# The opening of a fused linear-attention and two-layer kernel: weight tiles loaded and decoded earlier, the first block's products moved behind the last attention units

## The chip, the cores and the metric

One core of one Trainium2 chip. The metric is the device time of one execution in microseconds (us). The kernel before took 906.34, 907.86 and 909.46 us in three runs; the median is 907.86 us.

## The reference

Decayed linear attention over 4 sequences, 8 heads, 768 positions, 64 per head; its rows go through two layers, each with a nonlinearity between two matrix products.

```
for t in range(S):
    state = gamma * state + einsum('bhd,bhe->bhde', k[:, :, t], v[:, :, t])
    y[:, :, t] = scale * einsum('bhd,bhde->bhe', q[:, :, t], state)
x = y.transpose(0, 2, 1, 3).reshape(3072, 512)
h = x @ w_in                  # 512 x 2048
x = (h - tanh(h)) @ w_out     # 2048 x 512
h = x @ w_in2                 # 512 x 1024
solu = h * softmax(h)
out = layer_norm(solu) * g_ln @ w_out2
```

Weights arrive as float64 and are turned into float32 pairs (high and low part) on the core.

## The kernel before

**Attention.** Positions are cut into 6 chunks of 128; with 4 sequences that makes 24 units, number k = 4 x chunk + sequence. A unit has two input tiles of 512 KB, `z` (`load_half`, L194: first q and k, then k and v), which SP issues; SP also issues the weight tiles and the decay tables `tab` (L190). `prepare(k)` scales q on POOL (L223) and v partly on ACT (L230, one instruction a head) and partly on POOL (L234). `unit(ko, ks)` then does on PE the products "out" of unit ko and "sc" of unit ks (both L211, 64x64 matmuls), and on DVE and ACT what follows: the mask and the running state (L305, L311 to L316), the sum `xf` (ACT L277 to L281, DVE L285), and `split_x`, which cuts xf into a high part (ACT, L323) and a low part (DVE and POOL, L324).

**First layer.** Four units of one chunk make one block of 512 rows. `step_h(n, b)`, called h(n,b) here, multiplies column tile n of w_in (16 tiles) with block b: `products_h` issues 12 matmuls of 128x512 (L337), `less_tanh` follows (ACT L344, DVE L345). h(n,b) needs weight tile n, decoded, and all four units of block b.

**Decoding a weight tile.** `Decoder.to(stage, upto)`: stage 0 is the load (`raw`, 512 KB, L120), stage 1 an absolute value on ACT (L126), stage 2 four operations on DVE (L133, L134, L137, L140), stage 3 a copy on ACT (L149) and a subtraction on DVE (L150).

**What sets the order.** The code is written once, in program order, and a scheduler (in the tile framework) may move an instruction on its engine, except where `pin` keeps it in program order. Before, `pin` holds the unit matmuls, the first two blocks' h matmuls and some ACT copies of units 0 to 7. The matmuls of the opening stand on PE in this order: sc(0), sc(1), out(0), sc(2), out(1), sc(3), out(2), sc(4), out(3), sc(5), out(4), sc(6), h(0,0), out(5), sc(7), out(6), h(1,0), out(7), and then, without units between, h(0,1), h(1,1), h(2,0), h(2,1), h(3,0), h(3,1). From then on unit 8 to 11 (the third block) are strewn between the steps of the loop `for n in range(NF1)`, first sc(8), and after h(15,1) `products_y` (L362) starts on the second matrix. It needs `split_g(0)`, which cuts g of tile 0 into high (ACT, L350) and low part.

In the loop `for k in range(2 * B)` weight tile 0 is decoded in the code of units 1 and 2, tile 1 in that of units 4 and 5:

```
        if k in (1, 4):
            for st in (1, 2):
                dec1.to(st, 1 + (k > 1))
        elif k in (2, 5):
            dec1.to(3, 1 + (k > 2))
        if k in (4, 6):
            step_h((k - 4) // 2, 0)
```

Of the kernel before, what the change touches and what calls it, by code (L numbers as in the profile page):

```python
# [90 lines left out]
def body(ctx: ExitStack, tc, z, w_in, w_out, w_in2, w_out2, g_ln, cst, tab, out):  # L91
# [29 lines left out]
        return raw  # L121


    def stage1(raw):
        wf = t2([P, 512], F32, "wf")
        nc.scalar.activation(wf, raw[:, :, 1].bitcast(F32), AF.Abs)  # L126
        return wf

    def stage2(raw, wf):

        hw, lw = raw[:, :, 1], raw[:, :, 0]
        wb = wf.bitcast(I32)
        nc.vector.tensor_scalar(wf, wf, W_MIN, W_MAX, ALU.max, ALU.min)  # L133
        nc.vector.tensor_scalar(  # L134
            wb, wb, 3, 0x3FFFFFF8, ALU.logical_shift_left, ALU.bitwise_and
        )
        nc.vector.scalar_tensor_tensor(  # L137
            wb, lw, 29, wb, ALU.logical_shift_right, ALU.bitwise_or
        )
        nc.vector.scalar_tensor_tensor(  # L140
            wb, hw, -0x40000000, wb, ALU.bitwise_and, ALU.bitwise_or
        )

    def stage3(wf, scale, eng):
# [4 lines left out]
        nc.scalar.copy(hi, wf)  # L149
        eng.tensor_tensor(lo, wf, hi.bitcast(F32), ALU.subtract)  # L150
        return hi, lo

    class Decoder:
# [2 lines left out]
            self.at = [0] * 4  # L156
            self.raw, self.wf, self.w = {}, {}, {}

        def to(self, st, upto):
            while self.at[st] < min(upto, self.n):  # L160
                i = self.at[st]
                if st == 0:
                    self.raw[i] = raw_load(self.srcs[i])
                elif st == 1:
                    self.wf[i] = stage1(self.raw[i])
                elif st == 2:
                    stage2(self.raw.pop(i), self.wf[i])
                else:
                    self.w[i] = stage3(self.wf.pop(i), self.scales[i], self.eng)
                self.at[st] += 1  # L170

        def step(self):
# [40 lines left out]
    def prepare(k, own, wide=False):  # L213

        c = k // B
        if wide:
            t = t4([P, 2, H * D], F32, "vq")
            v = t[:, 0, :].rearrange("q (h d) -> q h d", h=H)
            qs[k] = t[:, 1, :].rearrange("q (p t) -> q p t", p=NP)
        else:  # L220
            v = t2([P, H, D], F32, "vs")
            qs[k] = t2([P, NP, P], F32, "qs")
        nc.gpsimd.tensor_tensor(  # L223
            qs[k].rearrange("q p t -> q (p t)"),
            zq[k][:, 0, :, :].rearrange("q p t -> q (p t)"), tb[c], ALU.mult,
        )
        src = zv[k][:, 1, :, :].rearrange("q p (h d) -> q (p h) d", h=2)
        c0 = C_VS + c * H
        for h in range(own):
            pin(nc.scalar.activation(  # L230
                v[:, h, :], src[:, h, :], AF.Copy, scale=con[:, c0 + h : c0 + h + 1]
            ), wide)
        if own < H:
            nc.gpsimd.tensor_tensor(  # L234
                v[:, own:, :], src[:, own:, :],
                con[:, c0 + own : c0 + H].unsqueeze(2).to_broadcast([P, H - own, D]), ALU.mult,
            )
        vs[k] = v

    def unit(ko, ks, hold=False, pool=ps_r, tag="r", engs=None, amid=None):  # L240
# [4 lines left out]
        if ko is not None:  # L245
# [36 lines left out]
            if amid:  # L282
                amid()
            for ab in steps:
                nc.vector.tensor_tensor(  # L285
                    xa[:, :, rows(ab)], xa[:, :, rows(ab)], ya[ab], ALU.add
                )
            if not hold:
                split_x(c, b, xf, engs or (nc.gpsimd, nc.gpsimd), amid)
        if ks is not None:  # L290
# [11 lines left out]
            ])  # L302
            pr = t2([P, 2, NP, D], F32, "pr")
            for h in range(2):
                nc.vector.tensor_tensor(  # L305
                    pr[:, h, :, :], sc[h], mask.unsqueeze(1).to_broadcast([P, NP, D]), ALU.mult
                )
# [10 lines left out]
    def split_x(c, b, xf, engs, fixed=False):  # L318
        if b == 0:
            xt[c] = [[t4([P, 2, SB], F32R, f"x{n}") for _ in range(2)] for n in "hl"]  # L320
        for h in range(2):
            xh, xl = (xt[c][n][h][:, :, b * P : (b + 1) * P] for n in range(2))
            pin(nc.scalar.copy(xh, xf[:, h, :, :]), fixed)  # L323
            engs[h].tensor_tensor(xl, xf[:, h, :, :], xh.bitcast(F32), ALU.subtract)  # L324


    gt = {}
# [88 lines left out]
    nc.scalar.dma_start(out=con, in_=cst[:, :C_IDENT])  # L416
    load_half(0, 1)
    loaded[0] = 1
    load_units(3)
    dec1.to(0, 1)  # L420
    load_units(6)
    dec1.to(0, 2)
    load_units(2 * B)
    for k in range(2):
        prepare(k, H // 2, True)
        unit(None, k, **spare)
    prepare(2, H // 2, True)

    def ahead(k):
# [3 lines left out]
    for k in range(2 * B):  # L433
        both = (nc.vector, nc.gpsimd) if k < 2 * B - 1 else (nc.vector, nc.vector)
        unit(
            k, k + 2 if k + 2 < 2 * B else None, engs=both,
            amid=lambda: ahead(k + 3), **spare
        )

        if k in (1, 4):  # L440
            for st in (1, 2):
                dec1.to(st, 1 + (k > 1))
        elif k in (2, 5):
            dec1.to(3, 1 + (k > 2))
# [29 lines left out]
    gs = {}  # L474

    def split_g(n):
        g = g2.pop(n)
        gs[n] = [split(g[:, b, :], nc.scalar, nc.vector) for b in range(2)]
# [213 lines left out]
```

## Time and profile before

| | us |
|---|---|
| median of three runs | 907.86 |
| the profiled execution | 906.58 |
| its span, first to last instruction | 904.8 |
| PE busy | 875.7 (97%) |
| DVE busy | 434.4 (48%) |
| ACT busy | 301.5 (33%) |
| POOL busy | 192.9 (21%) |

A row of the timeline has the start in us, the time from the start of the first to the end of the last of its instructions, the engine, the line, the operation, the tile written and those read, the shape and the count; in brackets the idle time of the engine before it and what ended it. "issue" there is time in which the engine waited for nothing that the profile shows. The table by stretch gives busy times (and the number of instructions) of PE, PE's weight loads (PEld), DVE, ACT and POOL, then the granted clock of PE, the mean busy share of the 16 DMA engines and GB/s. A row "q8" is the queue that the profile names "instruction".

### The profile page before, as it was taken

What the parts mean: (1) busy time and instruction counts of PE and PEld (TensorE: products, weight loads), DVE (VectorE), ACT (ScalarE), POOL (GpSimd) and SP (SyncE); (2) the same over time, 40 slices, a digit from 0 to 9 for tenths busy, and PEclk for the clock granted to TensorE, in tenths of its full rate; (3) what the DMA queues carried; (4) which work ended last, traced back from release to release, by engine and by line L of the source; (5) the groups of instructions that cost most, each with busy time, mean ns of one, the idle gap of its engine ahead of it and who ended that gap; (6) DMA issues with size and microseconds to landing.
All of it is one profiled execution on the core that took longest, in us unless ns stands there. A gap on an engine that the chain in (4) does not pass through costs nothing.

```text
span 904.8 us, 15888 instructions
## 1 busy us (share of the span) xinstructions
PE 875.7 (97%) x6656; PEld 723.9 (80%) x6656; DVE 434.4 (48%) x873; ACT 301.5 (33%) x606; POOL 192.9 (21%) x200
## 2 busy tenths in 40 slices
PE   4689999999999999999999999999999999999998
PEld 4577887888888887888788888888888888888886
DVE  2877857992232223222322269954544444444442
ACT  4446435551111111111111143622444333333332
POOL 4410000000233433333333210011222121222210
PEclk9799999999999999999999999999999999999999
DMA  9943104340312113110401055114111111100000
GB/s 360 342 168 120 35 24 158 98 137 27 94 67 75 60 47 94 48 47 7 134 6 44 24 151 175 48 35 129 47 36 38 44 47 46 36 24 24 24 24 35
DMA packets 34775, 71.93 MB, mean 79 GB/s; under 512 B 3088, under 2 KB 15504, under 8 KB 34704
## 3 DMA queue, kind: packets, MB, share of 16 engines
q1 hardware_dynamic: 18288, 58.01, 19.0%
q10 hardware_dynamic: 16416, 12.91, 4.5%
q8 instruction: 52, 0.85, 0.4%
q14 instruction: 19, 0.16, 0.1%
HBM read 58.32 MB, written 12.58 MB: 78 GB/s over the span
## 4 chain that ended last, share of the span: by engine, by line
PE 93%; DMA 3%; DVE 1%; issue 1%; ACT 1%; POOL 1%; SPq 0%; POOLq 0%; ACTq 0%
PE ph L337 29%; PE py L362 29%; PE po L616 15%; PE ph L568 14%; PE ptr L603 2%; PE out L211 2%; PE sc L211 2%; DMA z<-z 2%; DMA y1d<-ysb 1%; POOL qs L223 0%; DVE xl L324 0%; POOL vs L234 0%; DVE wf L140 0%; DVE w L150 0%; ACT th L344 0%
## 5 line engine op out<-in xcount | busy, mean ns | idle before, releaser
L362 PE MATMUL py<-gh,w 128*128 128x512 f32 x768 | 248.8, 392 | 1.2 <-ACT gh L350 1.2
L337 PE MATMUL ph<-xh,w 128*128 128x512 f32 x768 | 247.8, 392 | 2.0 <-ACT xh L323 2.0
L337 PEld LDWEIGHTS ph<-xh,w 128*128 128x128 f32 x768 | 145.1, 189 | 32.9 <-ACT xh L323 2.2
L362 PEld LDWEIGHTS py<-gh,w 128*128 128x128 f32 x768 | 143.4, 188 | 31.8 <-ACT gh L350 1.6
L345 DVE TENSOR_TENSOR g<-ph,th 128x512 f32<-128x512 f32 x96 | 66.3, 691 | 183.7 <-ACT th L344 183.7
L337 PE MATMUL ph<-xl,w 128*128 128x512 f32 x384 | 150.3, 391 | 0.3 <-DVE xl L324 0.3
L362 PE MATMUL py<-gl,w 128*128 128x512 f32 x384 | 149.8, 390 | 0.0
L344 ACT ACTIVATE th<-ph 128x512 f32<-128x512 f32 x96 | 57.3, 598 | 264.4 <-PE ph L337 248.9
L568 PE MATMUL ph<-w,y 128*128 128x512 f32 x576 | 134.9, 389 | 0.0
L353 POOL TENSOR_TENSOR gl<-g,gh 128x512 fp32r<-128x512 f32 x48 | 61.8, 1287 | 334.8 <-DVE gh L352 301.2
L568 PEld LDWEIGHTS ph<-w,y 128*128 128x128 f32 x576 | 108.1, 188 | 22.4
L616 PE MATMUL po<-w,uh 128*128 128x512 f32 x384 | 120.4, 395 | 0.0
L397 POOL TENSOR_TENSOR y<-yl,y 128x512 fp32r<-128x512 f32 x24 | 42.2, 1760 | 260.9 <-ACT y L396 232.5
L574 DVE TENSOR_REDUCE nmx<-ph 128x1 f32<-128x1024 f32 x24 | 29.4, 1225 | 117.7 <-PE ph L568 117.7
L337 PEld LDWEIGHTS ph<-xl,w 128*128 128x128 f32 x384 | 72.5, 189 | 15.5 <-DVE xl L324 0.6
L362 PEld LDWEIGHTS py<-gl,w 128*128 128x128 f32 x384 | 72.1, 188 | 14.9
L616 PEld LDWEIGHTS po<-w,uh 128*128 128x128 f32 x384 | 70.6, 188 | 13.6
L616 PE MATMUL po<-w,ul 128*128 128x512 f32 x192 | 75.3, 392 | 0.0
L577 ACT ACTIVATE ex<-ph,nmx 128x1024 f32<-128x1024 f32 x24 | 26.8, 1117 | 132.5 <-DVE nmx L574 132.5
L579 DVE SCALAR_TENSOR_TENSOR ex<-ph,ex 128x1024 f32<-128x1024 f32 x24 | 29.4, 1225 | 29.8 <-ACT ex L577 29.8
L616 PEld LDWEIGHTS po<-w,ul 128*128 128x128 f32 x192 | 36.0, 188 | 7.6
L149 ACT CAST w<-wf 128x512 fp32r<-128x512 f32 x48 | 29.6, 618 | 29.6 <-DVE wf L140 29.4
(76 smaller groups left out, 844.4 us busy)
## 6 DMA issues: line engine op xcount, KB each, us to landing
z<-z SPq DMA_DIRECT2D x48, 512.0 KB, 5.2
raw<-w_in SPq DMA_DIRECT2D x24, 512.0 KB, 5.0
raw<-w_out SPq DMA_DIRECT2D x24, 512.0 KB, 3.7
y1d<-ysb ACTq DMA_DIRECT2D x24, 256.0 KB, 3.5
yl<-y1d SPq DMA_DIRECT2D x24, 256.0 KB, 3.2
out<-ob ACTq DMA_DIRECT2D x24, 256.0 KB, 2.2
tab<-tab SPq DMA_DIRECT2D x5, 256.0 KB, 4.1
tab<-tab ACTq DMA_DIRECT2D x1, 256.0 KB, 4.6
```

What stands on the lines that cost most here:

```text
L149: nc.scalar.copy(hi, wf)
L211: pin(nc.tensor.matmul(o, a, b, start=True, stop=True, skip_group_check=True))
L337: nc.tensor.matmul(ph, a[:, k, :], x, start=n == 0, stop=n == 3 * NK - 1), s < 2
L344: nc.scalar.activation(th, ph, AF.Tanh)
L345: nc.vector.tensor_tensor(g, ph, th, ALU.subtract)
L353: eng_l.tensor_tensor(gl_, g, gh.bitcast(F32), ALU.subtract)
L362: nc.tensor.matmul(py[e], a[:, cols], x, start=f == 0 and n == 0, stop=f == NF1 - 1 and n == 2)
L397: nc.gpsimd.tensor_tensor(yo, t, yh.bitcast(F32), ALU.subtract)
L568: nc.tensor.matmul(ph[:, half, :], a[:, k, :], b, start=n == 0, stop=n == 3 * NK - 1)
L574: nc.vector.tensor_reduce(nmx, phf, AX.X, ALU.max, negate=True)
L579: nc.vector.scalar_tensor_tensor(ex, phf, 1.0, ex, ALU.mult, ALU.mult, accum_out=us)
L616: nc.tensor.matmul(po, a[:, f, :], b, start=n == 0, stop=n == 3 * NF2 - 1)
```

## The change

- **SP:** both weight tiles are loaded right behind the z tiles of units 0 and 1 (before: tile 0 behind unit 2's, tile 1 behind unit 5's). Tiles 2 and 3 are loaded where they were, behind the last z tile and two tables.
- **Decoding** of tile 0 stands behind sc(1) and in the code of unit 0, that of tile 1 in the code of units 0 and 1. Tile 2 is decoded, now pinned, in the code of unit 7.
- **h(0,0) and h(1,0)** stand behind out(6) and out(7).
- **`pin`** now also holds the POOL operations, the DVE operations and the decoding of units 0 to 7, so that ACT, DVE and POOL keep the program order there, as PE does.
- **The third block:** `prepare(k + 1)` now stands behind `unit(k)`, and that of unit 8 one step earlier, at n = 2. The loads of its z tiles move with it.
- **`split_g(0)`** stands before h(15,·) and no longer behind h(15,1).

```diff
-        nc.gpsimd.tensor_tensor(
+        pin(nc.gpsimd.tensor_tensor(
             qs[k].rearrange("q p t -> q (p t)"),
             zq[k][:, 0, :, :].rearrange("q p t -> q (p t)"), tb[c], ALU.mult,
-        )
+        ), wide)
...
-                nc.vector.tensor_tensor(
+                pin(nc.vector.tensor_tensor(
                     xa[:, :, rows(ab)], xa[:, :, rows(ab)], ya[ab], ALU.add
-                )
+                ), amid)
...
-            engs[h].tensor_tensor(xl, xf[:, h, :, :], xh.bitcast(F32), ALU.subtract)
+            pin(engs[h].tensor_tensor(xl, xf[:, h, :, :], xh.bitcast(F32), ALU.subtract), fixed)
...
-    load_units(3)
-    dec1.to(0, 1)
-    load_units(6)
+    load_units(2)
     dec1.to(0, 2)
     load_units(2 * B)
     for k in range(2):
         prepare(k, H // 2, True)
         unit(None, k, **spare)
+    for st in (1, 2):
+        dec1.to(st, 1, True)
     prepare(2, H // 2, True)
...
-        if k in (1, 4):
-            for st in (1, 2):
-                dec1.to(st, 1 + (k > 1))
-        elif k in (2, 5):
-            dec1.to(3, 1 + (k > 2))
-        if k in (4, 6):
-            step_h((k - 4) // 2, 0)
-    for st, n in enumerate((4, 3, 3, 3)):
-        dec1.to(st, n)
+        if k == 0:
+            for st, n in ((3, 1), (1, 2), (2, 2)):
+                dec1.to(st, n, True)
+        elif k == 1:
+            dec1.to(3, 2, True)
+        elif k >= 2 * B - 2:
+            if k == 2 * B - 1:
+                dec1.to(0, 4)
+                for st in (1, 2, 3):
+                    dec1.to(st, 3, True)
+            step_h(k - (2 * B - 2), 0)
...
     for n in range(NF1):
         while dec1.at[3] < n + 1:
             dec1.step()
+        if n == NF1 - 1:
+            split_g(0)
         for b in range(2):
             if n > 1 or b:
                 step_h(n, b)
 
-        if LATER <= n <= LATER + B:
-            k = 2 * B + n - LATER
-            if n == LATER:
-                load_units(k + 1)
-                prepare(k, H)
-            load_units(min(k + 2, 3 * B))
-            if n < LATER + B - 1:
-                prepare(k + 1, H)
-            unit(k - 1 if n > LATER else None, k if n < LATER + B else None, True)
+        k = 2 * B + n - LATER
+        if 2 * B <= k <= 3 * B:
+            unit(k - 1 if k > 2 * B else None, k if k < 3 * B else None, True)
+        if 2 * B <= k + 1 < 3 * B:
+            load_units(min(k + 3, 3 * B))
+            prepare(k + 1, H)
...
-    split_g(0)
```

The queue of SP at the start, the rows of before with -, those of the change with + (z and raw are 512 KB each):

```order
-L194 DMA z<-z 128x1024 x6
-L120 DMA raw<-w_in 128x1024
-L194 DMA z<-z 128x1024 x2
+L194 DMA z<-z 128x1024 x4
+L120 DMA raw<-w_in 128x1024 x2
+L194 DMA z<-z 128x1024 x4
 L190 DMA tab<-tab 128x512
-L194 DMA z<-z 128x1024 x4
-L120 DMA raw<-w_in 128x1024
-L194 DMA z<-z 128x1024 x4
```

The z tiles of unit 2 now stand as seventh and eighth, behind two weight tiles; those of unit 3 one place later than before, those of units 6 and 7 where they were.

PE, the first rows that differ; they stand behind sc(6) and lead into out(5) (sa and sb are a unit's states):

```order
 L211 MATMUL out<-pr,vq 64x64 x16
 L211 MATMUL sc<-vq,z 64x64 x32
-L337 MATMUL ph<-xh,w 128x512
-L337 MATMUL ph<-xl,w 128x512
-L337 MATMUL ph<-xh,w 128x512 x2
-L337 MATMUL ph<-xl,w 128x512
-L337 MATMUL ph<-xh,w 128x512 x2
-L337 MATMUL ph<-xl,w 128x512
-L337 MATMUL ph<-xh,w 128x512 x2
-L337 MATMUL ph<-xl,w 128x512
-L337 MATMUL ph<-xh,w 128x512
 L211 MATMUL out<-vq,sa 64x64 x4
```

h(0,0) is gone from here and stands behind out(6), where h(1,0) was; h(1,0) now follows out(7) and runs into h(0,1). All other matmuls up to sc(8) keep their order.

ACT around the scalings of v for units 8 and 9 (vs, L230), before:

```order
L149 CAST w<-wf 128x512
L230 ACTIVATE vs<-z,con 128x64 x16
L126 ACTIVATE wf<-raw 128x512
L344 ACTIVATE th<-ph 128x512 x2
L230 ACTIVATE vs<-z,con 128x64 x8
L277 COPY xc<-out 128x256 x2
```

and with the change:

```order
L149 CAST w<-wf 128x512 x2
L230 ACTIVATE vs<-z,con 128x64 x8
L126 ACTIVATE wf<-raw 128x512
L344 ACTIVATE th<-ph 128x512 x2
L230 ACTIVATE vs<-z,con 128x64 x8
L149 CAST w<-wf 128x512
```

The sixteen scalings in a row are parted: unit 8's eight stand two tanh (L344, one per h) ahead of unit 9's.

## Rows read from the trace of the kernel before

**Rows 1.** Table by stretch: from:to, length, busy times, clock, DMA share, GB/s.

```profile
15.75:21.80 6.05, 2.76 (x126) 2.45 (x127) 1.85 (x5) 4.01 (x16) 4.44 (x6) 1.00 1.03 407
21.80:27.99 6.19, 3.36 (x127) 3.17 (x126) 5.93 (x8) 1.39 (x5) 5.10 (x5) 0.72 1.02 394
27.99:32.08 4.09, 3.21 (x111) 2.83 (x111) 3.03 (x6) 3.63 (x15) 3.29 (x4) 0.63 0.52 122
32.08:40.85 8.77, 8.74 (x268) 7.74 (x268) 7.32 (x20) 4.92 (x16) 1.47 (x2) 0.78 0.96 381
```

**Rows 2.** Timeline of PE: where it resumes after being idle in the opening.

```profile
15.76 0.29 PE L211 MATMUL sc<-vq,z 64*64 64x64 f32 x4 [1.61 <-issue]
21.81 0.28 PE L211 MATMUL sc<-vq,z 64*64 64x64 f32 x3 [3.00 <-issue]
28.00 0.28 PE L211 MATMUL out<-vq,sb 64*64 64x64 f32 x4 [2.83 <-issue]
32.09 0.38 PE L211 MATMUL out<-vq,sb 64*64 64x64 f32 x4 [0.86 <-DVE sb L313]
44.81 0.29 PE L211 MATMUL out<-vq,sb 64*64 64x64 f32 x4 [3.99 <-issue]
```

**Rows 3.** The page: PE's instructions; the queue q8 (packets, MB, share).

```profile
PE 875.7 (97%) x6656; PEld 723.9 (80%) x6656; DVE 434.4 (48%) x873; ACT 301.5 (33%) x606; POOL 192.9 (21%) x200
...
q8 instruction: 52, 0.85, 0.4%
```

**Rows 4.** DMA queues in 19.3:19.4, 29.1:29.2 and 36.4:36.5 us (share of 16 engines).

```profile
q8 instruction: 1, 0.02, 64.1%
...
q8 instruction: 1, 0.02, 86.5%
...
q8 instruction: 1, 0.02, 61.8%
```

**Rows 5.** The chain of waits: start, us, what.

```profile
45.86 4.54 PE ph L337 x12
50.40 1.11 PE out L211 x64
...
54.31 16.41 PE ph L337 x71
```

**Rows 6.** Timeline of SP.

```profile
23.06 6.83 SPq L190 DMA_DIRECT2D tab<-tab  x2
29.94 3.75 SPq L120 DMA_DIRECT2D raw<-w_in  x6
```

**Rows 7.** Timeline of POOL and ACT: scalings that wait for z tiles.

```profile
10.63 1.27 POOL L223 TENSOR_TENSOR vq<-z,tab 128x512 f32<-128x512 f32 x1 [0.67 <-DMA z<-z]
15.99 1.27 POOL L223 TENSOR_TENSOR vq<-z,tab 128x512 f32<-128x512 f32 x1 [3.47 <-DMA z<-z]
28.27 1.27 POOL L223 TENSOR_TENSOR vq<-z,tab 128x512 f32<-128x512 f32 x1
17.23 1.06 ACT L230 ACTIVATE vq<-z,con 128x64 f32<-128x64 f32 x4 [2.87 <-DMA z<-z]
```

**Rows 8.** Timeline of PE around sc(8) and sc(9), and ACT's row before sc(8).

```profile
70.63 0.69 PE L211 MATMUL sc<-qs,z 64*64 64x64 f32 x32
72.20 2.01 PE L211 MATMUL sc<-vs,z 64*64 64x64 f32 x32 [0.88 <-ACT vs L230]
74.14 0.50 PE L337 MATMUL ph<-xh,w 128*128 128x512 f32 x1
...
80.78 0.66 PE L211 MATMUL sc<-qs,z 64*64 64x64 f32 x32
...
81.84 0.50 PE L337 MATMUL ph<-xh,w 128*128 128x512 f32 x1
...
71.80 3.93 ACT L230 ACTIVATE vs<-z,con 128x64 f32<-128x64 f32 x16
```

**Rows 9.** Timeline of PE: the first matmul on the second matrix.

```profile
149.18 1.20 PE L362 MATMUL py<-gh,w 128*128 128x512 f32 x4 [1.19 <-ACT gh L350]
```

More of the change, by code (lines that the diff above doesn't have):

```diff
@@ L121, in raw_load, with stage1, stage2, stage3 @@
         return raw
-    def stage1(raw):
+    def stage1(raw, fixed):
         wf = t2([P, 512], F32, "wf")
-        nc.scalar.activation(wf, raw[:, :, 1].bitcast(F32), AF.Abs)
+        pin(nc.scalar.activation(wf, raw[:, :, 1].bitcast(F32), AF.Abs), fixed)
         return wf
-    def stage2(raw, wf):
+    def stage2(raw, wf, fixed):
         hw, lw = raw[:, :, 1], raw[:, :, 0]
         wb = wf.bitcast(I32)
-        nc.vector.tensor_scalar(wf, wf, W_MIN, W_MAX, ALU.max, ALU.min)
-        nc.vector.tensor_scalar(
+        pin(nc.vector.tensor_scalar(wf, wf, W_MIN, W_MAX, ALU.max, ALU.min), fixed)
+        pin(nc.vector.tensor_scalar(
             wb, wb, 3, 0x3FFFFFF8, ALU.logical_shift_left, ALU.bitwise_and
-        )
-        nc.vector.scalar_tensor_tensor(
+        ), fixed)
+        pin(nc.vector.scalar_tensor_tensor(
             wb, lw, 29, wb, ALU.logical_shift_right, ALU.bitwise_or
-        )
-        nc.vector.scalar_tensor_tensor(
+        ), fixed)
+        pin(nc.vector.scalar_tensor_tensor(
             wb, hw, -0x40000000, wb, ALU.bitwise_and, ALU.bitwise_or
-        )
-    def stage3(wf, scale, eng):
+        ), fixed)
+    def stage3(wf, scale, eng, fixed):
         w = t4([P, 2, 512], F32R, "w")
@@ L148, in stage3 @@
             nc.scalar.activation(wf, wf, AF.Copy, scale=scale)
-        nc.scalar.copy(hi, wf)
-        eng.tensor_tensor(lo, wf, hi.bitcast(F32), ALU.subtract)
+        pin(nc.scalar.copy(hi, wf), fixed)
+        pin(eng.tensor_tensor(lo, wf, hi.bitcast(F32), ALU.subtract), fixed)
         return hi, lo
@@ L157, in __init__, with to @@
             self.raw, self.wf, self.w = {}, {}, {}
-        def to(self, st, upto):
+        def to(self, st, upto, fixed=False):
             while self.at[st] < min(upto, self.n):
@@ L164, in to @@
                 elif st == 1:
-                    self.wf[i] = stage1(self.raw[i])
+                    self.wf[i] = stage1(self.raw[i], fixed)
                 elif st == 2:
-                    stage2(self.raw.pop(i), self.wf[i])
+                    stage2(self.raw.pop(i), self.wf[i], fixed)
                 else:
-                    self.w[i] = stage3(self.wf.pop(i), self.scales[i], self.eng)
+                    self.w[i] = stage3(self.wf.pop(i), self.scales[i], self.eng, fixed)
                 self.at[st] += 1
@@ L222, in prepare @@
             qs[k] = t2([P, NP, P], F32, "qs")
-        nc.gpsimd.tensor_tensor(
+        pin(nc.gpsimd.tensor_tensor(
             qs[k].rearrange("q p t -> q (p t)"),
             zq[k][:, 0, :, :].rearrange("q p t -> q (p t)"), tb[c], ALU.mult,
-        )
+        ), wide)
         src = zv[k][:, 1, :, :].rearrange("q p (h d) -> q (p h) d", h=2)
@@ L233, in prepare @@
         if own < H:
-            nc.gpsimd.tensor_tensor(
+            pin(nc.gpsimd.tensor_tensor(
                 v[:, own:, :], src[:, own:, :],
                 con[:, c0 + own : c0 + H].unsqueeze(2).to_broadcast([P, H - own, D]), ALU.mult,
-            )
+            ), wide)
         vs[k] = v
@@ L284, in unit @@
             for ab in steps:
-                nc.vector.tensor_tensor(
+                pin(nc.vector.tensor_tensor(
                     xa[:, :, rows(ab)], xa[:, :, rows(ab)], ya[ab], ALU.add
-                )
+                ), amid)
             if not hold:
@@ L304, in unit @@
             for h in range(2):
-                nc.vector.tensor_tensor(
+                pin(nc.vector.tensor_tensor(
                     pr[:, h, :, :], sc[h], mask.unsqueeze(1).to_broadcast([P, NP, D]), ALU.mult
-                )
+                ), amid)
             pt[ks] = pr
@@ L438, in body, with split_g @@
         )
-        if k in (1, 4):
-            for st in (1, 2):
-                dec1.to(st, 1 + (k > 1))
-        elif k in (2, 5):
-            dec1.to(3, 1 + (k > 2))
-        if k in (4, 6):
-            step_h((k - 4) // 2, 0)
-    for st, n in enumerate((4, 3, 3, 3)):
-        dec1.to(st, n)
+        if k == 0:
[9 more added lines that the diff above has]
+            step_h(k - (2 * B - 2), 0)
     nc.sync.dma_start(out=gl, in_=g_ln)
+    gs = {}
+    def split_g(n):
+        g = g2.pop(n)
+        gs[n] = [split(g[:, b, :], nc.scalar, nc.vector) for b in range(2)]
     for n in range(NF1):
@@ L473, in body @@
                 dec1.to(st, max(NF1 if st < 3 else min(NF1, n + 2), NF1 + ahead[m]))
[L474 to L478, printed above, removed]
-    split_g(0)
     dec1.to(0, NF1 + 4)
```

## The prediction

> **What bounds the kernel now.** I read the page first: PE is busy for 97% of the span [rows 3]. A change of order can only win where PE idles, or works below its full clock of 2.4 GHz (granted 0.63 to 0.78 between 21.8 and 40.85 us, so partly at 1.2 GHz [rows 1]), and both stand before 54 us. From 54.31 us on, 71 matmuls of 128x512 run without a break [rows 5]. So the question is when that unbroken stretch begins, and what is left open behind it.
>
> The chain of waits names the decoding of tile 0 on DVE between 24 and 30 us, and one expects that moving it frees those 6 us. The timeline of PE says otherwise. It stops four times for "issue", that is, for no semaphore: it resumes at 15.76, 21.81, 28.00 and 44.81 us after 1.61, 3.00, 2.83 and 3.99 us, 11.4 us in all [rows 2]. For DVE it waits once, 0.86 us, until 32.09 [rows 2]. The table by stretch tells what the four stops have in common. From 15.75 to 21.80 PE and PEld start 126 + 127 instructions, from 21.80 to 27.99 127 + 126, and from 27.99 to 40.85, over two stretches, 222 + 536 = 758, which is three times 253 [rows 1]. The page has 6656 + 6656 of them and 52 packets of the queue "instruction", 0.85 MB: 256 to a packet [rows 3]; the few that are missing from 253 are PE's waits, which are not counted. So PE's program comes in blocks of 256 instructions by the same 16 DMA engines that carry z and w_in, and PE stops where a block is not there yet.
>
> The time for one block can be read. The block that PE resumed with at 15.76 us was the last it had; the next packet starts in 19.3:19.4 and takes 64.1% of 0.1 us x 16 engines = 1.03 us [rows 4], so it ends at 20.4, and PE goes on at 21.81, 1.4 us later. Wait of 3.6, packet 1.03, 1.4 until it runs: 6.05 us, and 6.19 for the next [rows 1]. That is with the DMA engines full (share 1.03, 1.02). After 28.00 they are half empty (share 0.52) [rows 1], and the packet starts in 29.1:29.2, after 1.1 us, and takes 86.5% = 1.38 us [rows 4]: 1.1 + 1.38 + 1.4 = 3.9 us. The following block is entered just after 32.09, and its packet starts at 36.4 and takes 61.8% = 0.99 us: 4.3 + 0.99 + 1.4 = 6.7 us, the longest, with the loads of w_in tiles (from 29.94 us [rows 6]) in front of it [rows 4]. So a block costs 6.1 us behind a full DMA, 3.9 behind a quiet one.
>
> The Trainium skill ("Runtime: NRT & Kernel Launch", "Instruction fetch mechanics") says that instructions come in 16 KiB blocks of 256 by a DMA queue of the sequencer, and calls the cost of crossing into a block mostly hidden. The size agrees with [rows 3]; hidden it is not in [rows 2]. What the time would be if it were hidden is the third rival.
>
> **The change, part by part.** Units 0 to 7 need about the same number of blocks in any order, so I follow the blocks.
>
> 1. *Two weight tiles ahead of unit 2.* Unit 2's q half landed ahead of 10.63, unit 3's ahead of 15.99 [rows 7]. The tiles land in the order of the queue, so unit 2's second half now takes the place of unit 3's q half, 15.95 us. The second block is entered within sc(2), at the product that needs unit 2's fourth scaling on ACT; four take 1.06 us [rows 7], so at 17.05 instead of 15.76: **+1.3 us on the chain of blocks**.
> 2. *The next blocks.* 17.05 + 6.1 + 6.1 = 29.25 us: the bytes ahead of the last z tile are the same, so the DMA goes quiet where it did (share 0.52 from 27.99 on [rows 1]), and now stays quiet for longer. SP's second table waits for the slot that POOL's scaling for unit 7 frees. Before, that scaling ran at 28.27 [rows 7], the second table was out by 29.9 and the w_in tiles went from 29.94 [rows 6]. Now POOL keeps program order, so unit 7's scaling stands behind the low parts of units 2 and 3 (L324), which wait for out(2) and out(3), that is for the blocks entered at 23.15 and 29.25. I put the w_in loads at about 35 us. So two blocks at 3.9: 33.1 and 37.0 us. The sixth is asked for at 37.0, 2 us after those loads start: 6.1 us, **43.1 us**; bounds 3.9 (40.9 us) and 6.7 (43.7 us). Before, this block came at 44.81.
> 3. *h(0,0) and h(1,0).* As now for h(1,0), the rest of the out products takes 1.05 us (44.81 to 45.86), then h(0,0) runs, out(7) 1.11, h(1,0), and h(0,1) begins. Twelve matmuls take 2.77 us in the unbroken stretch (16.41 / 71 each) and took 4.54 behind the idle of 3.99 us [rows 5]; as PE idles as long again, I take 4.54 for h(0,0) and 2.77 for h(1,0), which also covers the chain of unit 7 (51.51 to 54.31 before). 43.1 + 1.05 + 4.54 + 1.11 + 2.77 = 52.6 us. Before, the stretch of 72 began, in effect, one matmul ahead of 54.31, at 54.1. **Gain 1.5 us**; bounds: 40.9 and h(0,0) at 2.77 gives 48.6, gain 5.5; 43.7 gives 53.2, gain 0.9.
> 4. *Decoding.* Tile 0 now is turned while DVE waits for unit 2's z, tile 1 beside units 0 and 1; neither has a reader before 43 us. Nothing on the path: the 0.86 us that DVE held PE at 32.09 [rows 2] is within the wait for the block. Tile 2 is needed at h(2,0), 5.5 us after h(0,1) begins; its load comes some 10 us before. Its ACT and DVE operations, some 5 us with the two tanh steps among them, start with the end of unit 7's chain, so they fit with little to spare; if not, the cost is that difference.
> 5. *Unit 8.* Now sc(8) takes from 70.63 to 74.14, 3.5 us, and sc(9) from 80.78 to 81.84, 1.06 us [rows 8]: sc(8) stops 0.88 us for ACT and then goes at the pace of 16 scalings in 3.93 us [rows 8]. With eight of them one step earlier they lie beside h matmuls: **gain 2.45 us**. Bound below: 0.88 alone if ACT is late again.
> 6. *split_g(0) earlier.* PE waits 1.19 us for gh [rows 9]. Ahead of h(15,·) the split has 5.5 us of cover. **Gain 1.2 us.**
> 7. *Order held on ACT, DVE, POOL.* It costs what stands behind a waiting instruction; the only place where I see this decide is POOL's scaling in step 2, and there it delays SP's w_in loads, which have time.
>
> Sum: 1.5 + 2.45 + 1.2 = 5.15 us. Against the profiled execution, 906.58 - 5.15 = 901.4; against the median of 907.86, 902.7. The profiled run lies low in the three (906.34 to 909.46); I take 902.0.
>
> **The rivals.**
>
> - *The sixth block is asked for before the w_in loads fill the engines*, and h(0,0) may run at the unbroken pace. For it: the table and the loads start within some 2 us of the request, either side. Gain 5.5 with both (3.7 with the first alone), in all 7.4 to 9.2 us: about 899.
> - *Nothing of the opening is won:* the two blocks from 29 to 37 us cost 6.1, because other bytes keep the engines busy. 17.05 + 5 x 6.1 = 47.55 us, 2.75 after now's 44.81 instead of 1.7 before it: h(0,1) at 57.0, loss 2.9, less 3.65 for steps 5 and 6: 905.8 to 907.1, no change. Against it: share 0.52 in the stretch that follows the last z [rows 1].
> - *The blocks are hidden after all* and "issue" was something that the new order does not meet. Then the last z tile bounds: unit 7's scaling can't end before 29.5, two blocks of PE work behind it at the pace of 32.08 to 40.85 less h(0,0) (about 2.8 us each [rows 1]) give 35.2 in place of 43.1: 7.9 us more, 894.
> - *Slower:* the two weight tiles in front put PE behind by one block's place, and every block up to h(0,0) then costs the longest 6.7 us [rows 4]: 17.05 + 5 x 6.7 = 50.55, h(0,1) at 60.0, loss 5.9 less 3.65 = 2.3, against the median 910.1. It decides from 6.2 us a block on (each tenth is 0.5 us); above 6.8 it would be plainly slower. For it: one block did cost 6.7. Against: four did not.
>
> **How the numbers follow.** A measurement here can tell 0.3%, 2.7 us. My forecast has 0.5, the first rival 0.27, the hidden blocks 0.04, nothing won 0.13, slower 0.06. The range reaches from the first rival's better end (907.86 - 9.2 less what the runs spread, 897) to the third case (906): it leaves out the hidden blocks, the slower case and the ends. Faster by over 0.3% (below 905.1) is the forecast, the first rival and the hidden blocks, with a little of the forecast's upper end lost: 0.8. Same 0.15, slower 0.05.
>
> **What would show it.** PE resumes after "issue" at about 17, 23, 29, 33, 37 and 43 us, with 253 counted instructions between; SP issues w_in tiles 2 and 3 near 35 us, not 30; h(0,0) starts near 44 and h(0,1) near 52; sc(8) takes about 1 us and no gap stands before the first L362. Wrong is the account of the opening if PE's stops end with a semaphore of DVE, POOL or ACT, if their distance is not 256 instructions, or if h(0,1) begins before 47 or after 55 us.

## The result and the profile after

| | before | after |
|---|---|---|
| median, us | 908.44 (4 runs, 906.34 to 909.46) | 900.16 (4 runs, 898.75 to 900.99) |
| ratio, 95% interval | | 0.991 [0.9887, 0.9933] |
| profiled execution, us | 906.58 | 900.99 |
| its span, us | 904.8 | 899.2 |

The kernel became 8.3 us faster by the medians (6 to 10 us by the interval) and 5.6 by the profiled executions. The forecast was 902.0 in a range from 897 to 906. The page of after has the same instructions and the same 52 packets of PE's program as [rows 3]; only PE's span has shrunk.

```profile
span 899.2 us, 15890 instructions
...
PE 874.1 (97%) x6656; PEld 723.5 (80%) x6656; DVE 434.1 (48%) x873; ACT 301.4 (34%) x606; POOL 193.8 (22%) x200
...
q8 instruction: 52, 0.85, 0.4%
```

The timeline of PE in the opening of after, the rows with idle time ahead of them, answers to [rows 2]:

```profile
14.75 1.23 PE L211 MATMUL sc<-vq,z 64*64 64x64 f32 x32 [2.35 <-POOL vq L223]
16.14 1.52 PE L211 MATMUL sc<-vq,z 64*64 64x64 f32 x29 [0.16 <-ACT vq L230]
22.52 0.28 PE L211 MATMUL sc<-vq,z 64*64 64x64 f32 x3 [1.89 <-issue]
27.32 0.38 PE L211 MATMUL out<-vq,sb 64*64 64x64 f32 x9 [2.82 <-ACT sb L311]
28.87 0.38 PE L211 MATMUL out<-vq,sb 64*64 64x64 f32 x4 [1.16 <-issue]
35.96 0.27 PE L211 MATMUL out<-vq,sa 64*64 64x64 f32 x1 [0.41 <-issue]
41.95 0.37 PE L211 MATMUL out<-vq,sa 64*64 64x64 f32 x2 [3.87 <-issue]
```

The table by stretch between these rows, with the columns of [rows 1]: PE and PEld start 127 + 126, twice 254 and 126 + 127 instructions, so 253, two times 254, and 253, as the blocks of 256 want it. The two blocks from 28.87 cost 7.09 us together with the DMA engines at a share of 0.06, the next one 5.99 us at 0.98. PE is busy for 6.60 of the 7.09 us, at a granted clock of 0.60, so these two blocks lie near PE's own pace; the price of a quiet block is read better from the second execution of this kernel (after2, below).

```profile
22.52:28.87 6.35, 2.37 (x127) 2.10 (x126) 5.52 (x11) 3.68 (x15) 2.95 (x4) 0.91 0.93 355
28.87:35.96 7.09, 6.60 (x254) 6.28 (x254) 5.13 (x15) 5.50 (x22) 5.70 (x7) 0.60 0.06 18
35.96:41.95 5.99, 2.13 (x126) 1.99 (x127) 4.16 (x12) 1.66 (x5) 1.46 (x2) 0.95 0.98 339
41.95:49.72 7.77, 7.77 (x121) 6.25 (x120) 1.60 (x4) 1.96 (x5) 2.02 (x2) 0.60 1.02 408
```

The chain of waits of after, which answers to [rows 5] and [rows 8]: h(0,0) from 43.50 at a low clock, out(7), and then 84 matmuls (h(1,0), and h(0,1) to h(3,1)) without a break up to sc(8), which now takes 1.09 us.

```profile
38.09 3.87 issue
41.95 1.54 PE out L211 x31
43.50 5.13 PE ph L337 x12
48.63 1.09 PE out L211 x64
49.72 19.28 PE ph L337 x84
69.00 1.09 PE sc L211 x64
```

sc(8) stands at 69.00 where it stood at 70.63 [rows 8]: 1.63 us are won ahead of it. The h matmuls behind it go on at 70.09 in place of 74.14: 2.4 us more. From there to the first L362 it is 73.51 us (70.09 to 143.60, row below) in place of 75.04 (74.14 to 149.18): 1.5 us less, of which 1.19 are the wait for gh [rows 9]. Behind that both take 755.6 us to the end. 1.6 + 2.4 + 1.5 = 5.6 us, all of it.

```profile
143.60 1.52 PE L362 MATMUL py<-gh,w 128*128 128x512 f32 x6
```

SP's queue in after, which answers to [rows 6]: the w_in tiles go out at 35.21 us.

```profile
22.88 12.28 SPq L190 DMA_DIRECT2D tab<-tab  x2
35.21 2.33 SPq L120 DMA_DIRECT2D raw<-w_in  x5
```

### The profile page after: what moved, and what is told of

Read it like the earlier page. It is cut to its first block, busy times and chain, and to the rows that moved or that the text cites. A ratio compares the mean times of both kernels' runs of the same rounds, so it can differ in the third digit from the quotient of the medians.

```text
span 899.2 us, 15890 instructions
## 1 busy us (share of the span) xinstructions
PE 874.1 (97%) x6656; PEld 723.5 (80%) x6656; DVE 434.1 (48%) x873; ACT 301.4 (34%) x606; POOL 193.8 (22%) x200
## 4 chain that ended last, share of the span: by engine, by line
PE 94%; DMA 2%; issue 1%; DVE 1%; ACT 1%; POOL 1%; ACTq 0%; POOLq 0%
PE ph L337 29%; PE py L362 29%; PE po L616 15%; PE ph L568 15%; PE out L211 3%; PE ptr L603 2%; PE sc L211 2%; DMA z<-z 1%; DMA con<-cst 1%; DMA y1d<-ysb 0%; POOL qs L223 0%; POOL vs L234 0%; DVE g L345 0%; ACT th L344 0%; DVE w L150 0%
## 5 line engine op out<-in xcount | busy, mean ns | idle before, releaser
L362 PE MATMUL py<-gh,w 128*128 128x512 f32 x768 | 248.8, 392 | 0.0
L362 PEld LDWEIGHTS py<-gh,w 128*128 128x128 f32 x768 | 143.3, 188 | 30.4 <-ACT gh L350 0.2
L362 PE MATMUL py<-gl,w 128*128 128x512 f32 x384 | 149.8, 390 | 0.0
L344 ACT ACTIVATE th<-ph 128x512 f32<-128x512 f32 x96 | 57.3, 598 | 258.9 <-PE ph L337 245.9
L362 PEld LDWEIGHTS py<-gl,w 128*128 128x128 f32 x384 | 72.1, 188 | 14.9
L353 DVE TENSOR_TENSOR gl<-g,gh 128x512 fp32r<-128x512 f32 x48 | 33.8, 707 | 10.1 <-PE py L362 8.1
```

Of the source, the lines that this page charges most:

```text
L344: nc.scalar.activation(th, ph, AF.Tanh)
L353: eng_l.tensor_tensor(gl_, g, gh.bitcast(F32), ALU.subtract)
L362: nc.tensor.matmul(py[e], a[:, cols], x, start=f == 0 and n == 0, stop=f == NF1 - 1 and n == 2)
```

## The experiments

The theory: PE's program comes in blocks of 256 instructions by the DMA engines that carry z and w_in, and the gain of the opening comes from when those engines are quiet. The main rival: PE waits for data (tile 0's decoding, unit 7's chain), and the weight tiles that come earlier are what is won. p_unit8, p_split, p_open and a_h0 ran on one chip, after2, a_dup, a_quiet and a_both on a second, a_nopin, a_loads and a_best on a third, a_ql apart from these; the kernel before ran beside each group, and kernels of different groups are compared by their ratios to it. In the tables and timelines of kernels with added lines, the line numbers shift by one or two.

**The three parts alone.** Each kernel has one part of the change.

p_unit8, the kernel before with the new order of the third block:

```diff
-            load_units(min(k + 2, 3 * B))
-            if n < LATER + B - 1:
-                prepare(k + 1, H)
-            unit(k - 1 if n > LATER else None, k if n < LATER + B else None, True)
+            unit(k - 1 if k > 2 * B else None, k if k < 3 * B else None, True)
+        if 2 * B <= k + 1 < 3 * B:
+            load_units(min(k + 3, 3 * B))
+            prepare(k + 1, H)
```

> The kernel before with only the third block's order of the change (prepare behind the unit, unit 8's one step earlier). Theory: sc(8) takes about 1.06 us instead of 3.5, the opening stays as before (PE's stops of the opening at the same times within 0.3 us): 2.45 us less than the kernel before. Rival (the moved loads and scalings collide with the decoding of the w_in tiles): only the 0.88 us that sc(8) waited for ACT, or less.

Measured: ratio 0.9979 [0.9969, 0.9989], 1.9 us less. sc(8) starts both halves 0.51 us apart and has no wait:

```profile
70.71 0.69 PE L211 MATMUL sc<-qs,z 64*64 64x64 f32 x32
71.22 0.65 PE L211 MATMUL sc<-vs,z 64*64 64x64 f32 x32
```

The opening, though the same as before's, does not repeat within the 0.3 us that I expected: its stops end at 16.15, 22.42, 28.69 and 45.06 us, 0.25 to 0.7 us behind [rows 2]. So much can two executions differ there.

p_split, the kernel before with split_g(0) ahead of h(15,·):

```diff
+        if n == NF1 - 1:
+            split_g(0)
...
-    split_g(0)
```

> The kernel before with only split_g(0) ahead of h(15,.). Theory: the 1.19 us wait for gh ahead of the first L362 is gone and nothing else moves: 1.2 us less than the kernel before. Rival (the split delays tanh and the subtraction of h(14,.), so that PE waits for a free ph there): 0 us, with a new gap of PE ahead of h(15,.).

Measured: ratio 0.9993 [0.9983, 1.0004]: 0.6 us less, with 1.2 and 0 both inside the interval. Its trace has the first L362 at 147.86 us in place of 149.18, directly behind the h matmuls, which gives the theory's size; the medians can't tell it from nothing.

p_open, the changed kernel with these two undone:

```diff
-        if n == NF1 - 1:
-            split_g(0)
...
-        if 2 * B <= k + 1 < 3 * B:
-            load_units(min(k + 3, 3 * B))
-            prepare(k + 1, H)
+            load_units(min(k + 2, 3 * B))
+            if n < LATER + B - 1:
+                prepare(k + 1, H)
+            unit(k - 1 if n > LATER else None, k if n < LATER + B else None, True)
```

> The change without its parts for the third block and split_g: the opening alone. Theory (the prediction's sum): 1.5 us less than the kernel before; h(0,1) begins near 52.5 us, sc(8) takes 3.5 us and PE waits 1.2 us ahead of the first L362 as before. Rival (the opening is worth what the medians leave once 3.65 us are taken from 8.3): 4.6 us less, with PE at work earlier than the profile of the changed kernel shows.

Measured: ratio 0.9991 [0.9979, 1.0003], 0.8 us less; its profiled execution is 1.9 us longer than that of before. The rival's 4.6 us lie outside the interval; the theory's 1.5 lie inside it, so the medians alone can't tell them from nothing. The trace can: the opening is as in the changed kernel (the stretch of 84 matmuls begins at 49.78), yet nothing of it is left at the end, and sc(8), for which the theory had 3.5 us, takes 4.95 (69.05 to 74.00). The timeline of PE shows where it goes:

```profile
69.05 0.69 PE L211 MATMUL sc<-qs,z 64*64 64x64 f32 x32
71.92 2.16 PE L211 MATMUL sc<-vs,z 64*64 64x64 f32 x32 [2.18 <-ACT vs L230]
74.00 0.79 PE L337 MATMUL ph<-xh,w 128*128 128x512 f32 x1
```

PE is at sc(8) 1.6 us earlier, but ACT gains only 0.3: it starts the 16 scalings of v for units 8 and 9 at 71.52 (before: 71.80 [rows 8]), behind a copy that waits for DVE's decoding. So PE goes on at 74.00, where it went on at 74.14, and the longer stop of 2.18 us is followed by a lower clock: granted 0.53 (so mostly 1.2 GHz) from 74 to 79 us, where before had 1.00. The same stretch in both tables, p_open's:

```profile
74.00:79.00 5.00, 5.00 (x15) 3.96 (x13) 3.65 (x8) 2.01 (x8) 0.00 (x0) 0.53 0.00 0
```

and that of before:

```profile
74.00:79.00 5.00, 5.00 (x27) 4.12 (x27) 4.08 (x10) 2.89 (x10) 0.00 (x0) 1.00 0.00 0
```

What the opening wins was kept only together with the third block's new order. The parts do not add: alone they give 0.8 + 1.9 + 0.6 = 3.3 us, together 8.3.

**The change again**, unedited, as the measure for a_dup, a_quiet and a_both, which ran beside it:

> The changed kernel once more, beside the next three. If the three parts (opening, third block, split_g) add up as the prediction had it, it stands 3.3 us below the kernel before, the sum of what the three showed alone (0.8, 1.9 and 0.6 us). If the opening alone had lost its gain at sc(8), where PE then waited 2.18 us for vs and afterwards ran h matmuls at the lower clock, and the third block's part gives that back, it stands 5.5 to 8.5 us below.

Measured: 899.67 us, ratio 0.9909 [0.9894, 0.9925], 8.3 us less than before: the parts need each other. This profiled execution took 899.68 us, 1.31 less than the first one, and the trace says where: the packet of the sixth block, which stood in 39.5:39.6 us in the first, stands in 38.4:38.5, and PE resumes at 40.65, not 41.95; everything behind keeps these 1.3 us. The queue in these two windows, in the first execution:

```profile
q8 instruction: 1, 0.02, 58.2%
```

and in the second:

```profile
q8 instruction: 1, 0.02, 60.0%
```

In its timeline of PE each block of the opening shows as a stop:

```profile
28.67 0.28 PE L211 MATMUL out<-vq,sb 64*64 64x64 f32 x4 [0.85 <-issue]
32.24 0.26 PE L211 MATMUL out<-vq,sa 64*64 64x64 f32 x1 [0.47 <-issue]
35.75 0.27 PE L211 MATMUL out<-vq,sa 64*64 64x64 f32 x1 [1.03 <-issue]
40.65 0.37 PE L211 MATMUL out<-vq,sa 64*64 64x64 f32 x2 [2.77 <-issue]
```

The table by stretch between them prices two quiet blocks, both ended by a stop, at 3.57 and 3.51 us, and the sixth at 4.90:

```profile
28.67:32.24 3.57, 3.10 (x126) 2.80 (x127) 2.82 (x8) 3.20 (x14) 2.84 (x4) 0.65 0.08 27
32.24:35.75 3.51, 2.47 (x128) 2.33 (x127) 2.68 (x8) 2.75 (x10) 3.19 (x5) 0.87 0.02 5
35.75:40.65 4.90, 2.13 (x127) 1.99 (x128) 4.06 (x12) 1.50 (x5) 1.46 (x2) 0.93 0.90 312
```

SP's loads of w_in go out at 35.34 us, 0.41 us ahead of the sixth block's entry at 35.75; in the first execution at 35.21, 0.75 us ahead of 35.96:

```profile
35.34 2.46 SPq L120 DMA_DIRECT2D raw<-w_in  x5
```

**a_dup: one more block.** The products of sc(3) issued more often:

```diff
-            ])
+            ] * (2 if ks == 3 else 1))
...
-            ])
+            ] * (4 if ks == 3 else 1))
```

> The change with the products of sc(3) issued again with the same result: 16 of the first list twice, 16 of the second four times, so 256 more PE instructions (128 MATMUL, 128 weight loads). Block theory: one more block lies ahead of h(0,0); PE's stop before it ends 6.1 us later if the DMA is full behind it, 3.9 if it is quiet, so h(0,1) begins 3.9 to 6.1 us later and the kernel is as much slower than the changed one, with one more packet of the instruction queue ahead of 42 us. Rival (PE's stops have to do with its data, and instructions cost only their time on PE): at most the 2.8 us that 128 such matmuls run, less where PE stood idle anyway: 0 to 2.8 us slower.

Measured: 904.17 us, 4.5 more than the change beside it. The stop ahead of h(0,0) ends at 45.24 in place of 40.65, 4.6 later. Of these, 3.5 us are the added block (the last block ahead of h(0,0) is entered at 39.25 in place of 35.75), and 1.1 us are that last block, which costs 5.99 us and not 4.90; in the first execution of the change it also took 5.99. The table by stretch (the first row holds two blocks, in which PE is busy for 6.20 of 7.00 us at a clock of 0.65) prices a block of 253 to 255 counted instructions at 3.58 us with quiet engines, at 5.99 with full ones:

```profile
28.67:35.67 7.00, 6.20 (x254) 6.05 (x254) 4.41 (x12) 5.19 (x20) 2.54 (x3) 0.65 0.04 14
35.67:39.25 3.58, 2.11 (x128) 1.98 (x127) 3.06 (x10) 2.40 (x9) 2.95 (x4) 1.00 0.12 30
39.25:45.24 5.99, 2.13 (x126) 1.99 (x127) 3.50 (x11) 1.36 (x4) 1.05 (x2) 0.88 0.98 350
```

In the last two rows PE is busy for 2.1 us of the 3.58 and of the 5.99: it is not the instructions' own time. The rival's bound of 2.8 us at most is passed both by the medians (4.5) and by the added block alone (3.5), whose instructions run in 2.1.

**a_quiet: the engines kept quiet for the sixth block.** The load of w_in tile 2 waits for a small memset of its buffer, which POOL does behind unit 5's low part:

```diff
+        if late:
+            pin(nc.gpsimd.memset(raw[:, 0, :].bitcast(F32), 0.0))
...
+        elif k == 2 * B - 3:
+            dec1.to(0, 3)
```

> The change with w_in tiles 2 onward held back until POOL has written the low part of unit 5's x (a small POOL memset of tile 2's buffer stands ahead of its load), so from about 40 us instead of 35.2. Block theory: the sixth block, asked for at 36 us, now finds the DMA engines quiet and costs 3.9 instead of 6 us: PE resumes at 39.9 instead of 41.95, h(0,1) begins some 2.1 us earlier, 2.1 us less than the changed kernel (bounds 1 and 3.5). Rival (the wait has nothing to do with the DMA engines): PE resumes at 42 as before, no change or a loss, since the weight tiles come 5 us later.

Measured: 896.84 us, ratio to before 0.9875 [0.9858, 0.9892], 2.8 us less than the change beside it. The loads start at 39.54, PE resumes at 39.25 after 1.95 us. The block costs 4.07 us:

```profile
35.18:39.25 4.07, 2.13 (x126) 1.99 (x127) 3.27 (x10) 1.91 (x6) 1.41 (x3) 1.00 0.25 68
39.25:44.14 4.89, 4.89 (x121) 3.98 (x120) 2.43 (x7) 1.96 (x5) 1.00 (x3) 1.00 0.78 249
```

Only 1.4 us of the gain over the execution beside it is the earlier end of the stop: 0.8 the block's price (4.07 for 4.90), 0.6 that PE enters it at 35.18 and not 35.75, ahead of anything that the memset changes. The rest is the second row: from PE's return to the start of h(1,0) it takes 4.89 us at a granted clock of 1.00, where the first execution of the change took 7.77 us at 0.60 (last row of its table by stretch) and the one beside it 7.73, also at 0.60: 2.8 us less. Of the waits for weight tiles that a later load could bring, 0.14 us came (DVE's low part of a tile, until 58.63).

**a_h0 and a_both: h(0,0) in its old place.** a_h0:

```diff
-        elif k >= 2 * B - 2:
-            if k == 2 * B - 1:
...
-            step_h(k - (2 * B - 2), 0)
+        elif k == 4:
+            step_h(0, 0)
+        elif k == 2 * B - 1:
...
+            step_h(1, 0)
```

> The change with h(0,0) back ahead of out(5), h(1,0) left behind out(7). Block theory: h(0,0) then holds 24 of a block's 256 instructions and runs in time in which PE otherwise waits for a block; PE enters the blocks at the same times (stops that end near 28.9 and 42 us), so that h(0,1) begins earlier by some 2.9 us, the h(0,0) that ran behind the stop less what is then slow in h(1,0): 2.9 us less than the changed kernel (bounds 1.5 and 4.5). Rival (PE has no idle room there, or the low part of unit 3's x is late for h(0,0) and holds up the units): no gain, or a loss of up to 2 us.

Measured: ratio to before 0.9906 [0.9889, 0.9924], the change's own; by the traces 0.9 to 2.2 us less than the two executions of the change. The expectation was too high, since I had the blocks entered at the same times. h(0,0) runs at the full clock, 2.94 us, but the boundary lies behind it: of the block entered at 33.09, 251 instructions have started by 38.00 us, so the next one is entered there and not near 36, and the stop ends at 42.55. One block later PE stops once more, 0.76 us until 48.63. The table by stretch has for the block entered at 33.09:

```profile
33.09:38.00 4.91, 4.91 (x124) 4.07 (x127) 4.19 (x12) 2.38 (x10) 3.49 (x5) 0.96 0.29 95
```

a_both is a_h0 with the memset of a_quiet:

```diff
         elif k == 4:
             step_h(0, 0)
+        elif k == 2 * B - 3:
+            dec1.to(0, 3)
```

> h(0,0) ahead of out(5) and w_in tiles 2 onward held back, together. Block theory: the block asked for at 36.4 us is there at 40.3, when PE has just used up the one before; the stop of 2.34 us that a_h0 kept is gone or under 0.5 us: 2.2 us less than with h(0,0) moved alone, 3.7 to 4.5 less than the changed kernel. Rival (the two gains are the same idle time, and unit 5's or 6's data bound next): no more than the better of the two alone.

Measured: 897.66 us, 2.0 less than the change and no less than a_quiet (0.8 more, with runs that overlap): as the rival has it, no more than the better of the two. The edit held back less than it was meant to: one w_in tile still goes out at 35.29 us, the others behind the memset at 41.05. The stop shrank to 1.49 us, ending at 40.69, and then PE waited for the decoding of tile 3, whose steps DVE mixes with those of two other tiles. The timeline of PE:

```profile
58.71 0.50 PE L339 MATMUL ph<-xh,w 128*128 128x512 f32 x1 [1.41 <-ACT w L151]
60.20 0.73 PE L339 MATMUL ph<-xh,w 128*128 128x512 f32 x2 [0.76 <-DVE w L152]
```

a_best adds to a_both a pinned decoding of tile 3 right behind tile 2:

```diff
             for st in (1, 2, 3):
                 dec1.to(st, 3, True)
+            for st in (1, 2, 3):
+                dec1.to(st, 4, True)
```

> h(0,0) ahead of out(5) and the w_in loads held back, as in a_both, with tile 3 decoded right behind tile 2 on ACT and DVE, in program order. In a_both PE then stood 1.41 and 0.76 us for tile 3's high and low part, since DVE worked at three tiles at once. Theory: both waits are gone: 2 to 3 us less than a_both, near 895 us at a kernel before of 907.7. Rival (DVE is full from 47 us on, and what tile 3 gains tiles 4 and 5 or g lose): the wait moves to h(4,0), no gain.

Measured: ratio to before 0.9904 [0.9886, 0.9922], no gain, a miss: the waits for tile 3 are gone, and PE waits 0.54 us for DVE's g at 60.82 and 0.93 us for vs at sc(8), whose second half again takes 2.01 us. With the stops shorter, what DVE and ACT have to do before sc(8) reads as the next limit; no run tests it.

**a_nopin: the pins that the change added, taken out** (on POOL, DVE and in the decoding):

```diff
-        pin(nc.gpsimd.tensor_tensor(
+        nc.gpsimd.tensor_tensor(
...
-            pin(engs[h].tensor_tensor(xl, xf[:, h, :, :], xh.bitcast(F32), ALU.subtract), fixed)
+            engs[h].tensor_tensor(xl, xf[:, h, :, :], xh.bitcast(F32), ALU.subtract)
...
         def to(self, st, upto, fixed=False):
+            fixed = False
```

> The change without the pins that it added (POOL's, DVE's and the decoding's; the scheduler then puts POOL's scaling for units 5, 6 and 7 ahead of the low parts of units 2 to 6). Block theory: unit 7's scaling runs as soon as its z is there, near 28.5 us, the second table and then w_in tiles 2 onward go out near 30 instead of 35.2 us, and the two blocks that cost 3.9 us in the quiet stretch from 29 to 36 us cost up to 6.1: PE's stop before h(0,0) ends up to 4.4 us later than in the changed kernel, which is then 2 to 4.4 us slower. Rival, as the prediction had it (the held order costs or gives nothing): within 1 us of the changed kernel.

Measured: 906.85 us, ratio to before 0.9988 [0.9977, 1.0]: without the pins nearly nothing is left, some 7 us of the 8.3 are gone. POOL scales for unit 7 at 28.27, not 33.53 as in the change (the line is L224 here):

```profile
28.27 1.26 POOL L224 TENSOR_TENSOR vq<-z,tab 128x512 f32<-128x512 f32 x1
```

SP's loads of w_in go out at 29.93:

```profile
29.93 2.41 SPq L120 DMA_DIRECT2D raw<-w_in  x5
```

and in the table by stretch the last blocks ahead of h(0,0) cost 6.05 and 6.20 us with full engines:

```profile
30.60:35.22 4.62, 3.89 (x136) 3.72 (x137) 3.00 (x9) 4.28 (x18) 1.09 (x2) 0.59 0.99 346
35.22:41.27 6.05, 2.12 (x128) 1.98 (x127) 4.04 (x12) 2.33 (x9) 1.46 (x2) 0.99 1.02 414
41.27:47.47 6.20, 3.59 (x126) 3.46 (x127) 2.50 (x7) 1.36 (x4) 0.73 (x1) 0.73 1.03 408
```

PE is released for h(0,0) at 47.47, 5.5 us behind the change's first execution: 2.5 us by the block of 6.05 that cost half of 7.09 there, 0.2 by the next, 2.8 ahead of them. Of these 2.8 us, by the count of instructions, 1.9 are that PE enters the block of the first row only at 30.8 (28.87 in the change), behind waits for ACT: 3.85 us for a scaling of v until 27.71, and 1.27 us for a state, in the timeline of PE:

```profile
30.60 0.70 PE L212 MATMUL out<-vq,sb 64*64 64x64 f32 x16 [1.27 <-ACT sb L312]
```

So some 3.6 of the 5.5 us are dearer blocks, and 1.9 are these waits. The run takes out all the pins together; what POOL's alone are worth it doesn't show. At h(0,0) 1.3 us come back, as it runs faster, so that the profiled spans differ by 4.2 us. The medians differ by more since a_nopin's profiled execution is the lowest of its twelve, 1.6 us below their median, and the change's first one the highest of its four, 0.8 above theirs; that makes 6.6 of some 7.

**a_loads: both weight tiles behind unit 3's z.**

```diff
-    load_units(2)
+    load_units(4)
     dec1.to(0, 2)
...
         if k == 0:
+            for st in (1, 2):
+                dec1.to(st, 1, True)
+        elif k == 1:
             for st, n in ((3, 1), (1, 2), (2, 2)):
                 dec1.to(st, n, True)
-        elif k == 1:
+        elif k == 2:
             dec1.to(3, 2, True)
```

> The change with both weight tiles loaded behind the z tiles of unit 3 instead of unit 1, and decoded one unit later. Theory: unit 2's z lands two tiles earlier, the block that PE entered at 22.5 us in the changed kernel is entered near 21.8 as before the change, and the later ones as much earlier: 0.7 to 1.3 us less than the changed kernel. Rival (the decoding now stands ahead of the units' work on DVE where it is tighter, and PE waits for DVE or ACT instead): no gain or up to 2 us more.

Measured: ratio to before 0.9877 [0.9857, 0.9897], 2.9 us less than the change, more than expected and for another reason. PE is released at 22.47 and 28.47, as in the change (22.52 and 28.87, again 22.47 and 28.67): the weight tiles ahead of unit 2 had cost these blocks next to nothing. The gain is at the sixth block, 4.08 us where the change had 5.99 and 4.90, and in h(0,0), which runs in 2.94 us at the full clock. SP's loads go out 0.7 us later:

```profile
35.93 3.15 SPq L120 DMA_DIRECT2D raw<-w_in  x5
```

and the table by stretch has for the block:

```profile
35.99:40.07 4.08, 2.13 (x126) 1.99 (x127) 3.40 (x10) 1.79 (x6) 1.47 (x3) 1.00 0.85 292
```

So the engines are not quiet in it (share 0.85), and yet it is cheap. What differs is how long the loads had been going out when PE entered the block: 0.06 us here, 0.41 and 0.75 us in the change (4.90 and 5.99 us), 0.97 us in a_dup (5.99 us); in a_quiet they started 4.4 us behind the entry (4.07 us). The block's packet starts 1.7 us after the entry here (in 37.6:37.7 us), 2.7 and 3.6 us after it in the change. These rows order themselves by what had been asked for ahead of the packet, not by the share of the whole stretch. No run varies this alone.

**a_ql: a_loads and a_quiet together**, so a_loads with

```diff
+        elif k == 2 * B - 3:
+            dec1.to(0, 3)
```

> a_loads with w_in tiles 2 onward held back as in a_quiet (until POOL has written the low part of unit 5's x). Theory: both gained at one and the same stop, the sixth block's, which ends at 39.25 and 40.07 us in them after 1.95 us, with h(0,0) at the full clock behind it; together it ends near 39.5 and the time is that of the better one, 896 to 897.5 us at a kernel before of 907.4. Rival (the gains add): 894 us, with the stop ending before 38.5.

Measured: ratio to before 0.9877 [0.9855, 0.99]; the stop ends at 39.76. The two gains are the same stop, as expected, and do not add. a_quiet and a_loads, about 897 us, lie below the kernel before and below the change (a_loads by its ratio, as it ran on another chip).

## Why the prediction was right, and where it was not

*What bounds.* Right. In the tables above, PE's returns from one stop to the next lie 252 to 255 counted instructions apart, or twice that where no stop shows between two blocks; an added block makes the kernel 4.5 us longer; and the price of a block goes from 3.5 us to 6.2 with what else the DMA engines have to carry. One reading was off: the block of 6.7 us, the upper bound, is entered at 32.47 us by the count of instructions and the next at 38.77, so it cost 6.3 at most. The Trainium skill ("Runtime: NRT & Kernel Launch", "Instruction fetch mechanics") calls a block's crossing mostly hidden; after's trace disagrees in the opening (stops of 0.41 to 3.87 us) and agrees from 42 us on, where PE's timeline has no such stop.

*Step 1, two weight tiles ahead of unit 2: +1.3 us.* Right about when the second block is entered, wrong about what follows from it. By the count of instructions PE enters it at 16.87 us, within sc(2)'s second half (16.14 in the timeline of after); predicted were 17.05, and before had 15.76. But the next block is there after 5.65 us and not 6.1, at 22.52 and not 23.15. The old opening in p_unit8 and p_split enters at 16.15 and 16.14 and goes on at 22.42 and 22.31; a_loads, with the tiles out of the way, at 16.11 and 22.47. By these rows the late entry cost the chain 0.2 us or less, by before's one trace (21.81) 0.7. The step went wrong in adding a fixed price to the entry: in these rows, with the DMA engines full, the next block came at nearly the same time, whether the one before it was entered at 16.1 or at 16.9 us.

*Step 2.* The w_in loads at 35.2 us (about 35 predicted) and the full price for the sixth block (5.99, predicted 6.1) are as forecast. The two quiet blocks cost 7.1 us together, 3.55 each (3.57 and 3.51 in after2), not 3.9. That is 0.7 us of the 1.15 by which PE is back earlier than predicted (41.95, not 43.1); 0.4 is step 1's. That the sixth block costs the full price is not a fixed fact of this kernel: the second execution had 4.90.

*Step 3.* Right in sum, by luck, as two errors cancel: PE came 1.15 us earlier than predicted, h(0,0) took 5.13 and not 4.54, and the rest of out ahead of it 1.54 and not 1.05. The gain ahead of sc(8) was 1.63 for 1.5 predicted.

*Step 4.* Right: no wait for tiles 0 to 2 stands on the path. DVE and ACT did hold PE up once (2.82 us for sb, until 27.32), behind tile 1's decoding on DVE, ahead of a block that came only at 28.87.

*Step 5.* The 2.45 us are there (2.4 in the trace, 1.9 by p_unit8). What the step missed is that it also carries step 3: with ACT's scalings left where they were, sc(8) waits 2.18 us, and p_open keeps almost nothing of the opening. That could be read before: in [rows 8] sc(8) waits 0.88 us for ACT, so its time was not PE's to set.

*Step 6.* 1.3 us in the trace for 1.2; by medians inside the noise.

*Step 7, the held order.* Its one effect was named, in step 2, as a date for SP's loads, but never priced. Of all parts it is the one whose loss costs most: without the pins 7 us of 8.3 are gone, and the time, 906.85, is that of the second rival (905.8 to 907.1), for the larger part by that rival's mechanism: other bytes keep the engines busy, and two blocks cost 6.05 and 6.20. Some 1.9 us ahead of them are waits for ACT, which neither the step nor the rival had.

*The size.* 5.15 us predicted, 5.59 between the profiled executions, 8.3 between the medians. The 8.3 lie above the forecast's size, and the difference from 5.59 is which executions were profiled: before's, 906.58, lies 1.9 us below the median of its four runs, after's, the highest of its four, 0.8 above. For the change two traces show what differs (the sixth block's packet and the end of that stop). For before there is one trace, and the place stays open; but of its 64 runs beside the experiments all below 907 us show a mean granted clock of 0.991 to 0.994 and all above 908 us one of 0.985 to 0.991, so its longer executions had PE at the lower clock for longer.

## What to carry to other kernels

Where PE is idle for "issue" at a steady count of instructions, what helped here is to have no large loads asked for just ahead of the next block's packet: hold back loads that have time, and see which engine's order decides when they go out. A gain at one place is only kept if the next thing that PE meets isn't set by another engine's clock: follow each gain to the next wait, and run the parts alone as well as together. One profiled execution can lie 1.3 us from another of the same kernel, so a sum of that size needs a second trace.

## What the runs showed of the hardware that I had not expected

- The same kernel, twice: one packet of PE's program that stands about 1.1 us earlier in the DMA queues comes with an end 1.3 us earlier (899.2 and 897.9 us of span). The loads of w_in had gone out 0.75 us ahead of the block's entry in one, 0.41 us in the other.
- What PE does after a stop can cost nearly as much again. Behind stops of 3.87 and 2.77 us (the change, twice), 2.61 us (a_nopin) and 2.12 us (a_ql) the twelve matmuls of h(0,0) took 5.13, 5.10, 4.28 and 4.54 us; behind 1.95 us (a_quiet and a_loads) PE worked at a granted clock of 1.00, and h(0,0) took 2.94 us in a_loads. p_open shows the same far from the opening, with no DMA at all (share 0.00): 2.18 us for vs, then 0.53.
- A block of 256 instructions costs PE more than its work even with nearly idle DMA engines: 3.58 us with 2.11 of them busy, at a DMA share of 0.12 (a_dup).
- The busy share of a stretch does not price the block in it: 4.08 us at a share of 0.85 (a_loads), 4.90 at 0.90 and 5.99 at 0.98 (the change), 4.07 at 0.25 (a_quiet).
